# Starting the second layer of the first chunk early, and another order of weight scaling, in a Fourier-filter and snake-MLP kernel

## The chip, the cores and the metric

The kernel runs on one core of one Trainium2 chip. The metric is the device time of one execution in microseconds (us). An execution with the hardware profiler on gives the trace that the views below come from.

Engines: PE is TensorE (matmuls; PEld its weight loads), DVE is VectorE, ACT is ScalarE, POOL is GpSimd, SP is SyncE, which here only issues DMAs.

## The reference

Eight sequences of 3008 rows and 256 columns are filtered in the frequency domain, and all 24064 rows then go through an MLP with the snake activation:

```python
X = np.fft.rfft(x, axis=1)
y = np.fft.irfft(X * (filt_r + 1j * filt_i)[None], n=3008, axis=1)
h = y.reshape(24064, 256) @ w_in            # d_ff = 2048
g = h + sin(alpha * h) ** 2 / (alpha + 1e-09)
out = g @ w_out                             # float32
```

## The kernel before, in words

**Fourier part.** 3008 = 47 x 64, so the transform is two stages of small DFT matrices. Batch 0 is done in the head (L441 to L585). Batches 1 to 7 are done piece by piece between the MLP's matmuls: `first` (L206, PSUM tile pa; its copy to SBUF, t_h, by ACT or DVE in rotation), a round through DRAM (d<-t_h by SP, then t<-d, the t2 tiles, by POOL), `forward` (L243, pb), the product with the filter, `inverse` (pc), a second round through DRAM, and `last` (pd), whose result is y. For batch 1 there are sixteen pieces of `first`, called pa 0 to pa 15 here, and t_h k is the copy of pa k. In the trace, pa 0, 3, 6 and 9 are copied by DVE, the other twelve by ACT. The last step of batch 0 (`last_0`, L407, also called pd) is partly left for later: its matmuls are put one by one between MLP matmuls by `one_between`.

**MLP.** The rows are cut into 48 chunks of 512 columns of y (one in twelve has 384), and d_ff into 16 blocks jb of 128. With 2 sin^2 = 1 - cos(2 ...), the activation becomes v = cos(ph) - 1 - ph, where w_in is scaled by alpha beforehand (`weights_in`, six pieces g on POOL, L547) and w_out by -1/(2 alpha) (`weights_out`, three pieces of four blocks on POOL, L581, and four of one block on ACT, L579).

- `hidden(k, jb)` makes one block: two matmuls of 512 columns into ph (L608), cos on ACT into cos_all (L612), v on DVE (L613). Names such as ph 8, cos 8 and v 8 mean block jb = 8. There are four buffers of ph and four of cos.
- `project(k, u)` is the second layer: u = (t, half), where t is one of four tiles of 128 rows and half is blocks 0 to 7 or 8 to 15. It is eight matmuls of 256 columns into po (L628). Two tiles t share a PSUM bank; when both are done, ACT copies them to o (L637) and POOL issues the stores (L673).

**Order.** Each engine runs its instructions in program order. The program goes in half steps: `step` counts pairs of hidden blocks, eight per chunk. In step j of chunk k it emits `hidden(k, 2j)` and `hidden(k, 2j+1)`, then the Fourier pieces that `put` has laid on this step (`slot`), then 1/8 of the previous chunk's `project`. So chunk 0 has no second-layer work of its own beside it, and chunk 1 carries that of chunk 0.

**Buffers that matter here.** `fps` has two PSUM buffers, for pa, pb, pc and pd; `hps` four, for ph; `ops` two, for po. `vpool` has two buffers of SBUF: w_out32, the raw w_out, lies in the one that becomes v of chunk 1. `opool` has three: the zero tile `idle`, which feeds the idle matmuls of `warm_pe`, whose results nothing reads, and later the output tiles o.

**POOL's queue** from 29 to 47 us: w_in pieces 0 to 2, x load 0 of batch 1, w_in 3, x 1, w_in 4, x 2, w_in 5, x 3, then w_out blocks 0 to 3, 4 to 7 and 8 to 11. Blocks 12 to 15 are scaled on ACT from step 5 of chunk 0.

Of the kernel before, what the change touches and what calls it, by code (L numbers as in the profile page):

```python
# [10 lines left out]
FP32 = mybir.dt.float32  # L11
# [3 lines left out]
ALU = mybir.AluOpType  # L15
# [3 lines left out]
B, S, C = 8, 3008, 256  # L19
# [52 lines left out]
def kernel(  # L72
# [10 lines left out]
    nc = tc.nc  # L83
# [31 lines left out]
    opool = pool("op", 3)  # L115
# [4 lines left out]
    ops = pool("ops", 2, PSUM)  # L120
# [13 lines left out]
    y = cpool.tile([128, 2, 2, 32, NR], FP16)  # L134
# [4 lines left out]
    for h in range(2):  # L139
        (nc.sync, nc.scalar)[h].dma_start(out=x32[:, 4 * C * h:4 * C * h + 4 * C],  # L140
                                         in_=bass.AP(tensor=x.tensor, offset=x.offset + 4 * h * C, ap=[[32 * C, 96], [1, 4 * C]]))
# [5 lines left out]
    w2 = cpool.tile([128, 16, C], FP16)  # L147
# [34 lines left out]
    def evac(dst, src, on_act=None):  # L182
        flip[0] = (flip[0] + 1) % 3
        if flip[0] if on_act is None else on_act:
            marks["act"] = nc.scalar.copy(out=dst, in_=src)  # L185
        else:
            marks["dve"] = nc.vector.tensor_copy(out=dst, in_=src)  # L187
# [161 lines left out]
    def spread_alpha(i):  # L349

        ps = hps.tile([128, 4, 128], FP32, name=f"al_bc_{i}", tag="h")
        for a in range(4):
            for k, part in enumerate(parts):
                nc.tensor.matmul(out=ps[:, a, :], lhsT=one[:, 4 * i + a:4 * i + a + 1].to_broadcast([128, 128]),
                                 rhs=part, start=(k == 0), stop=(k == 2))
        nc.scalar.copy(out=alpha[:, i // 2, 512 * (i % 2):512 * (i % 2) + 512], in_=ps.rearrange("p a b -> p (a b)"))

    for g in range(2):
        gs = slice(12 * g, 12 * g + 12)
        for k, filt in enumerate((filt_r, filt_i)):  # L360
            for q in range(2):
                if (g, k, q) == (0, 1, 1):
                    split_alpha()
                off, step = ((12 * g) * C, C) if q == 0 else ((N1 - 12 * g) * C, -C)
                marks["filt", g, k] = nc.gpsimd.dma_start(
                    out=f_t[k][64 * k + 32 * q:64 * k + 32 * q + 32, gs, :],
                    in_=bass.AP(tensor=filt.tensor, offset=filt.offset + off,
                                ap=[[N1 * C, 32], [step, 12], [1, C]]))
        if g == 1:
            nc.gpsimd.tensor_copy(out=f_t[0][64:128, 0:12].rearrange("p s c -> p (s c)").bitcast(UINT32),  # L370
                                  in_=f_t[0][0:64, 0:12].rearrange("p s c -> p (s c)").bitcast(UINT32))
        nc.gpsimd.dma_start(out=e_t[:, gs, :], in_=e_dram.ap()[:, gs])

    idle = opool.tile([128, 512], FP32, name="idle", tag="o")
    nc.vector.memset(idle, 0.0)
    idle = idle.bitcast(FP16)
# [11 lines left out]
    rec_t = cpool.tile([128, 16], FP32)  # L388
# [8 lines left out]
    def last_0(n0, n, own=fps, tag="f", spread=False):  # L397

        for cb in range(2):
            made = []  # L400

            def one(i, cb=cb, made=made):

                if i == 0:
                    ps = own.tile([128, 512], FP32, name=f"pd_0_{n0}_{cb}", tag=tag)
                    made.append(ps[:, 0:n * NR].rearrange("p (a r) -> p a r", r=NR))
                nc.tensor.matmul(out=made[0][:, i, :], lhsT=t4_cols[:, n0 + i, :, cb], rhs=wi0_t,  # L407
                                 start=True, stop=True)
                if i == n - 1:
                    evac(y[:, cb, 0, n0:n0 + n, :], made[0], cb == 0)  # L410

            for i in range(n):
                if spread:
                    between.append(lambda i=i, one=one: one(i))
                else:
                    one(i)
# [7 lines left out]
    def inverse_table(g):  # L424

        gs = slice(8 * g, 8 * g + 8)
        ps = ops.tile([128, 8, 128], FP16, name=f"pse_{g}", tag="o")
        for i in range(8):
            for a in range(2):
                nc.tensor.transpose(out=ps[64 * a:64 * a + 64, i, :],  # L430
                                    in_=d_t[:, 8 * g + i, 64 - 64 * a:128 - 64 * a], identity=id16)
        nc.scalar.mul(e1_0[:, gs, :], ps, -0.125)
# [3 lines left out]
    def warm_pe(n):  # L436

        warmed.append(n)
        ps = hps.tile([128, 512], FP32, name=f"warm_{len(warmed)}", tag="h")
        for i in range(n):  # L440
            nc.tensor.matmul(out=ps, lhsT=idle[:, 0:128], rhs=idle[:, 0:512], start=True, stop=True)  # L441
# [18 lines left out]
    for i in range(16):  # L460
# [7 lines left out]
        if i < 15 and i % 4 == 3:  # L468
            warm_pe((1, 2, 2, 1)[i // 4])
    spread_alpha(0)  # L470
    [inverse_table(g) for g in range(2)]
    spread_alpha(1)
    warm_pe((2, 2, 2, 1)[3])
# [63 lines left out]
    nc.sync.dma_start(out=wh_t, in_=wh_dram.ap())  # L537
    nc.sync.dma_start(out=wi_t, in_=wi_dram.ap())
    w_out32 = vpool.tile([128, 16, C], FP32, name="w_out32", tag="v")
    for jb in range(0, 16, 8):  # L540
        ins = nc.sync.dma_start(out=w_out32[:, jb:jb + 8],
                                in_=moe_w_out[128 * jb:128 * jb + 1024].rearrange("(b p) c -> p b c", p=128))
    s1 = Spectral(1)

    def weights_in(g):
# [29 lines left out]

    def weights_out(jb, n=4):

        if n == 1:
            nc.scalar.mul(w2[:, jb, :], w_out32[:, jb, :], rec_t[:, jb:jb + 1])  # L579
        else:  # L580
            nc.gpsimd.tensor_tensor(out=w2[:, jb:jb + n, :], in0=w_out32[:, jb:jb + n, :],  # L581
                                    in1=rec_t[:, jb:jb + n, None].to_broadcast([128, n, C]), op=ALU.mult)

    spread_alpha(2)
    spread_alpha(3)  # L585
    for step in ([(weights_in, g) for g in range(3)] + [(s1.load_x, 0), (weights_in, 3), (s1.load_x, 1),
                 (weights_in, 4), (s1.load_x, 2), (weights_in, 5), (s1.load_x, 3)]
                 + [(weights_out, jb) for jb in (0, 4, 8)]):
        step[0](*step[1:])
    warm_pe(12)  # L590
    last_0(0, 4)
# [6 lines left out]
    v = {}  # L598
    pso = {}

    def hidden(k, jb):

        _, c0, n = chunks[k]
        if jb == 0:
            v[k] = vpool.tile([128, 16, 512], FP16, name=f"v_{k}", tag="v")
        ps = hps.tile([128, 512], FP32, name=f"ph_{k}_{jb}", tag="h")
        for cb in range(2):
            nc.tensor.matmul(out=ps[:, 0:n], lhsT=w1[:, cb, jb * 128:jb * 128 + 128],  # L608
                             rhs=y_cols[:, cb, c0:c0 + n], start=(cb == 0), stop=(cb == 1))
            one_between()  # L610
        cs = cos_all[:, jb % 4, :]
        nc.scalar.activation(out=cs[:, 0:n], in_=ps[:, 0:n], func=AFT.Sin, bias=float(np.pi / 2))  # L612
        marks["snake"] = nc.vector.scalar_tensor_tensor(  # L613
            out=v[k][:, jb, 0:n], in0=cs[:, 0:n], scalar=-1.0, in1=ps[:, 0:n],
            op0=ALU.add, op1=ALU.subtract)

    def project(k, u):

        pb, c0, n = chunks[k]
        t, half = divmod(u, 2)  # L620
        rest = len(chunks) - 1 - k
        alone = rest == 0 or rest == 1 and t > 1
        if rest == 0 and t > 1:
            t = 5 - t
        if (t % 2 == 0 or alone) and half == 0:
            pso[k] = ops.tile([128, 2, C], FP32, name=f"po_{k}_{t}", tag="o")
        for jb in range(8 * half, 8 * half + 8):
            nc.tensor.matmul(out=pso[k][:, t % 2, :], lhsT=v[k][:, jb, 128 * t:128 * t + 128],  # L628
                             rhs=w2[:, jb, :], start=(jb == 0), stop=(jb == 15))
            if jb % 2:  # L630
                one_between()
        last = 128 * (t + 1) == n
        if half == 1 and (t % 2 == 1 or last or alone):
            i0 = t % 2 if alone else 0
            o = opool.tile([128, 2, C], FP32, name=f"o_{k}_{t}", tag="o")
            copy = nc.vector.tensor_copy if rest == 0 else nc.scalar.copy
            copy(out=o[:, i0:t % 2 + 1, :], in_=pso[k][:, i0:t % 2 + 1, :])  # L637
            for i in range(i0, t % 2 + 1):
                store(o[:, i, :], pb, c0 + 128 * (t - t % 2 + i),
                      (nc.scalar, nc.sync, nc.scalar, nc.scalar) if rest == 0 and t == 3 else  # L640
                      (nc.sync, nc.scalar) if rest == 0 or (rest == 1 and t > 2) else
                      (nc.sync,) if rest < 7 else (nc.gpsimd,))
# [36 lines left out]
    def put(at, fn, *args, pe=False):  # L679
        pending.append((at, len(pending), pe, fn, args))  # L680
# [20 lines left out]
    for at, fn in put_later:  # L701
        put(at, fn)

    for jb in range(12, 16):
        put(5 + 0.5 * (jb - 12), weights_out, jb, 1)

    for n0, n, at in ((6, 5, 1.5), (11, 4, 11), (15, 4, 13), (19, 4, 14.4), (23, 4, 15.6), (27, 5, 16.8)):
        put(at, last_0, n0, n, fps, "f", True)
    for b in range(1, B):
# [46 lines left out]
    step = 0  # L756
    for k in range(len(chunks) + 1):
        for j in range(8):
            if k < len(chunks) and step > 0:
                hidden(k, 2 * j)  # L760
                hidden(k, 2 * j + 1)
            slot(step)
            if k > 0:
                n_half = 2 * (chunks[k - 1][2] // 128)
                for u in range(n_half * j // 8, n_half * (j + 1) // 8):
                    project(k - 1, u)
            slot(step + 0.5)
            step += 1
# [31 lines left out]
```

## Time and profile before

| | us |
|---|---|
| three runs: median (lowest, highest) | 773.94 (773.56, 774.11) |
| the profiled execution, its own time | 773.78 |
| its span in the trace | 772.0 |
| PE busy in the span | 762.5 (99%) |
| DVE, ACT, POOL busy | 655.7, 610.4, 373.4 |
| first matmul of chunk 0 (L608) starts | 35.10 |
| first second-layer matmul (L628) starts | 46.85 |
| first forward matmul of batch 1 (L243) starts | 69.72 |

A group of the page stands for instructions of one line and tile: `L608 PE MATMUL ph<-y,w ... x1536` is the first layer. In a timeline a row gives start, duration from the first start to the last end, engine, line, operation, tiles and count; the brackets at its end give idle time of the engine just before, and what ended it. The ends of matmuls are modelled and overlap the next start, so spacing tells PE's rate better than the duration of one record.

### The profile page before, as it was taken

How to read it: one execution, taken by the hardware profiler on the slowest of the kernel's cores; microseconds unless marked ns; L12 is line 12 of the kernel's file. 1: busy time of each engine (PE TensorE's matmuls, PEld its weight loads, DVE VectorE, ACT ScalarE, POOL GpSimd, SP SyncE). 2: the span in 40 equal slices, each digit the busy share in tenths (PEclk: the TensorE clock that was granted, in tenths of full speed). 3: DMA queues.
4: the chain of work that ended last, by engine and by line, in shares of the span. 5: the costliest groups of instructions: out<-in, count | busy, mean ns of one | idle time of the engine just before them, and what ended most of it. 6: DMA issues, size and time to landing. Idle time of an engine off the chain costs nothing.

```text
span 772.0 us, 17226 instructions
## 1 busy us (share of the span) xinstructions
PE 762.5 (99%) x6038; PEld 516.8 (67%) x6038; DVE 655.7 (85%) x1171; ACT 610.4 (79%) x1205; POOL 373.4 (48%) x651
## 2 busy tenths in 40 slices
PE   8999999999999999999999999999999999999997
PEld 4757766666666667666666676766666666766666
DVE  6887998999989888988889988899888888777774
ACT  5898987898787878887878787888778787777763
POOL 7455456544546555555555646644464645430000
PEclk9999999999999999999999999999999999999999
DMA  9955679754855438654575536754254322511112
GB/s 225 288 108 171 139 168 265 199 131 111 222 141 128 118 85 212 141 122 111 121 194 117 135 94 155 200 141 123 70 147 110 88 70 55 138 45 33 40 37 61
DMA packets 81518, 101.49 MB, mean 131 GB/s; under 512 B 18884, under 2 KB 60864, under 8 KB 81431
## 3 DMA queue, kind: packets, MB, share of 16 engines
q0 software_dynamic: 27440, 47.29, 26.1%
q1 hardware_dynamic: 53426, 52.41, 25.7%
q8 instruction: 47, 0.77, 0.4%
q10 hardware_dynamic: 565, 0.70, 0.3%
q14 instruction: 40, 0.33, 0.1%
HBM read 56.15 MB, written 46.66 MB: 133 GB/s over the span
## 4 chain that ended last, share of the span: by engine, by line
PE 92%; DVE 3%; ACT 2%; DMA 1%; issue 1%; POOL 0%; POOLq 0%
PE po L628 41%; PE ph L608 41%; DVE v L613 3%; PE pd L316 2%; PE pb L243 2%; PE pa L222 2%; DMA w<-id 1%; PE pc L293 1%; ACT xf L499 1%; ACT cos_all L612 1%; PE pa L206 0%; PE pc L518 0%; ACT t_h L185 0%; PE pd L407 0%; PE warm L441 0%
## 5 line engine op out<-in xcount | busy, mean ns | idle before, releaser
L613 DVE SCALAR_TENSOR_TENSOR v<-cos_all,ph 128x512 f16<-128x512 f32 (+1 forms) x768 | 482.8, 672 | 95.3 <-ACT cos_all L612 91.6
L612 ACT ACTIVATE cos_all<-ph 128x512 f32<-128x512 f32 (+1 forms) x768 | 413.8, 599 | 98.9 <-PE ph L608 98.6
L673 POOL DMA_DIRECT2D out_dram<-o x530 | 292.7, 559 | 241.8 <-ACT o L637 213.8
L608 PE MATMUL ph<-y,w 128*128 128x512 f16 (+1 forms) x1536 | 389.0, 375 | 1.3 <-DVE v L613 1.1
L628 PE MATMUL po<-w,v 128*128 128x256 f16 x3008 | 389.4, 273 | 0.0
L628 PEld LDWEIGHTS <-v 128*128 128x128 f16 x3008 | 290.0, 98 | 84.4 <-issue 1.1
L608 PEld LDWEIGHTS <-w 128*128 128x128 f16 x1536 | 143.2, 98 | 113.4 <-issue 18.4
L637 ACT COPY o<-po 128x512 f32<-128x512 f32 (+1 forms) x95 | 56.1, 590 | 7.6 <-PE po L628 6.8
L185 ACT CAST y<-pd 128x376 f16<-128x376 f32 (+1 forms) x86 | 41.9, 489 | 12.8 <-PE pd L316 8.8
L246 ACT CAST xf<-pb 128x512 f16<-128x512 f32 x84 | 50.9, 606 | 1.3 <-PE ph L608 0.5
L160 POOL DMA_DIRECT2D x<-in_x_dram x48 | 25.7, 540 | 40.8 <-DVE v L613 26.6
L185 ACT CAST t_h<-pa 128x512 f16<-128x512 f32 (+1 forms) x60 | 32.8, 590 | 12.5 <-PE pa L222 11.3
L316 PEld LDWEIGHTS <-t_a 96*128 96x128 f16 x448 | 31.4, 97 | 12.7
L264 DVE TENSOR_TENSOR p<-p,xs 128x512 f16<-128x512 f16 x84 | 35.7, 425 | 2.9
L263 DVE TENSOR_TENSOR xs<-xs,filt_t 128x512 f16<-128x512 f16 x84 | 35.2, 419 | 1.8 <-DMA xs<-xf 1.7
L257 DVE TENSOR_TENSOR p<-xf,filt_t 128x512 f16<-128x512 f16 x84 | 35.1, 419 | 0.0
L185 ACT CAST gt<-pc 128x512 f16<-128x512 f32 x54 | 28.1, 594 | 8.4 <-PE pc L293 8.4
L187 DVE CAST t_h<-pa 128x512 f16<-128x512 f32 (+1 forms) x52 | 33.5, 683 | 0.2
L243 PE MATMUL pb<-t,d_t 128*128 128x256 f16 x168 | 32.1, 273 | 0.0
L316 PE MATMUL pd<-wh_t,t_a 96*128 96x94 f16 x384 | 31.8, 204 | 0.0
L235 POOL DMA_DIRECT2D t<-d x28 | 24.4, 874 | 10.8 <-DMA d<-t_h 9.4
L243 PEld LDWEIGHTS <-d_t 128*128 128x128 f16 x168 | 16.4, 98 | 14.3
(71 smaller groups left out, 275.3 us busy)
## 6 DMA issues: line engine op xcount, KB each, us to landing
t<-d POOLq DMA_DIRECT2D x28, 384.0 KB, 5.2
xs<-xf SPq DMA_DIRECT2D x168, 64.0 KB
t_a<-d SPq DMA_DIRECT2D x28, 384.0 KB
x<-in_x_dram POOLq DMA_DIRECT2D x50, 188.0 KB, 4.5
d<-t_h SPq DMA_DIRECT2D x48, 192.0 KB
d<-gt SPq DMA_DIRECT2D x36, 256.0 KB
out_dram<-o POOLq DMA_DIRECT2D x91, 64.0 KB, 2.1
out_dram<-o POOLq DMA_DIRECT2D x31, 80.0 KB, 3.6
```

What stands on the lines that cost most here:

```text
L185: marks["act"] = nc.scalar.copy(out=dst, in_=src)
L243: nc.tensor.matmul(out=ps[:, i, :], lhsT=d_t[:, s, :], rhs=self.t2[s // 6][:, s % 6, :], start=True, stop=True)
L246: nc.scalar.copy(out=self.xf[u], in_=ps)
L263: nc.vector.tensor_tensor(out=xs, in0=xs, in1=f_t[1][:, 2 * u:2 * u + 2, :], op=ALU.mult)
L264: nc.vector.tensor_tensor(out=p, in0=p, in1=xs, op=ALU.add)
L316: nc.tensor.matmul(out=psv[:, i, :], rhs=wi_t if self.b < TILED else wh_t, start=True, stop=True, lhsT=t4_h[ch // 2][0:NK, n0 % 16 + i, cb ...
L608: nc.tensor.matmul(out=ps[:, 0:n], lhsT=w1[:, cb, jb * 128:jb * 128 + 128], rhs=y_cols[:, cb, c0:c0 + n], start=(cb == 0), stop=(cb == 1))
L612: nc.scalar.activation(out=cs[:, 0:n], in_=ps[:, 0:n], func=AFT.Sin, bias=float(np.pi / 2))
L613: marks["snake"] = nc.vector.scalar_tensor_tensor(out=v[k][:, jb, 0:n], in0=cs[:, 0:n], scalar=-1.0, in1=ps[:, 0:n], op0=ALU.add, op1=ALU. ...
L628: nc.tensor.matmul(out=pso[k][:, t % 2, :], lhsT=v[k][:, jb, 128 * t:128 * t + 128], rhs=w2[:, jb, :], start=(jb == 0), stop=(jb == 15))
L637: copy(out=o[:, i0:t % 2 + 1, :], in_=pso[k][:, i0:t % 2 + 1, :])
L673: queues[i % len(queues)].dma_start(out=bass.AP(tensor=out.tensor, offset=out.offset + t0 * C, ap=[*ap, [1, C]]), in_=o_blk[p0:p0 + rows, :])
```

## The change

1. **Second layer of chunk 0.** 24 of its 64 matmuls (blocks 0 to 5, all four t) move into chunk 0: after each of `hidden(0, 7)` to `hidden(0, 14)` three of them are emitted. Both PSUM tiles po of chunk 0 are opened there, each by one matmul of zeros over the whole bank (512 columns), since two row tiles now accumulate in a bank by turns. In chunk 1 the rest, 40 matmuls, is emitted as 4, 4, 0, 8, 8, 0, 8, 8 in the eight steps instead of 8 in each. The first copy to o comes in step 4 instead of step 3.
2. **w_out.** All its blocks are scaled on POOL, between the w_in pieces and x loads; the last four come in two pieces of two blocks, from tiles of their own in `opool`. Nothing of it is on ACT. It is loaded by four DMAs instead of two.
3. **y.** Of the `last_0` piece n0 = 6, both copies to y are on ACT; before, one was on DVE.
4. **Head.** Six idle matmuls after the first `spread_alpha`.

```diff
@@ last_0
-                    evac(y[:, cb, 0, n0:n0 + n, :], made[0], cb == 0)
+                    evac(y[:, cb, 0, n0:n0 + n, :], made[0], cb == 0 or n0 == 6)
@@ head
     spread_alpha(0)
+    warm_pe(6)
     [inverse_table(g) for g in range(2)]
@@ loads of w_out
-    for jb in range(0, 16, 8):
-        ins = nc.sync.dma_start(out=w_out32[:, jb:jb + 8],
-                                in_=moe_w_out[128 * jb:128 * jb + 1024].rearrange("(b p) c -> p b c", p=128))
+    w_out_rest = [opool.tile([128, 2, C], FP32, name=f"w_out_{jb}", tag="o") for jb in (12, 14)]
+    for jb, n, dst in ((0, 8, w_out32[:, 0:8]), (8, 4, w_out32[:, 8:12]), (12, 2, w_out_rest[0]), (14, 2, w_out_rest[1])):
+        nc.sync.dma_start(out=dst, in_=moe_w_out[128 * jb:128 * (jb + n)].rearrange("(b p) c -> p b c", p=128))
@@ weights_out: always nc.gpsimd.tensor_tensor; the ACT form for n == 1 is gone
@@ POOL's order
-    for step in ([(weights_in, g) for g in range(3)] + [(s1.load_x, 0), (weights_in, 3), (s1.load_x, 1),
-                 (weights_in, 4), (s1.load_x, 2), (weights_in, 5), (s1.load_x, 3)]
-                 + [(weights_out, jb) for jb in (0, 4, 8)]):
+    for step in ([(weights_in, g) for g in range(4)]
+                 + [(weights_out, 0), (s1.load_x, 0), (weights_in, 4), (s1.load_x, 1), (weights_out, 4),
+                    (weights_in, 5), (s1.load_x, 2), (weights_out, 8), (s1.load_x, 3), (weights_out, 12, 2), (weights_out, 14, 2)]):
@@ new
+    early = [(t, jb) for jb in range(6) for t in range(4)]
+
+    def project_early(n):
+
+        for _ in range(min(n, len(early))):
+            t, jb = early.pop(0)
+            if (t % 2, jb) == (0, 0):
+                pso[0, t // 2] = ops.tile([128, 2, C], FP32, name=f"po_0_{t}", tag="o")
+                nc.tensor.matmul(out=pso[0, t // 2].rearrange("p t c -> p (t c)"), lhsT=idle[:, 0:128],
+                                 rhs=idle[:, 0:512], start=True, stop=False)
+            nc.tensor.matmul(out=pso[0, t // 2][:, t % 2, :], lhsT=v[0][:, jb, 128 * t:128 * t + 128],
+                             rhs=w2[:, jb, :], start=False, stop=False)
@@ project
-        for jb in range(8 * half, 8 * half + 8):
+        for jb in range(8 * half if k or half else 6, 8 * half + 8):
@@ scaling on ACT
-    for jb in range(12, 16):
-        put(5 + 0.5 * (jb - 12), weights_out, jb, 1)
@@ main loop
-                hidden(k, 2 * j)
-                hidden(k, 2 * j + 1)
+                for jb in (2 * j, 2 * j + 1):
+                    hidden(k, jb)
+                    if k == 0 and jb > 6:
+                        project_early(3)
             slot(step)
-            if k > 0:
+            if k == 1:
+                for u in ((0, 2), (4, 6), (), (1,), (3,), (), (5,), (7,))[j]:
+                    project(0, u)
+            elif k > 0:
```

## Prediction

> **What bounds the kernel now.** I read the page first, then a table of stretches, then the chain of waits and the engines' timelines from 33 to 70 us, where the change lies. Of the page, part 1 (busy time) and part 4 (the chain that ended last):
>
> ```profile
> PE 762.5 (99%) x6038; PEld 516.8 (67%) x6038; DVE 655.7 (85%) x1171; ACT 610.4 (79%) x1205; POOL 373.4 (48%) x651
> PE 92%; DVE 3%; ACT 2%; DMA 1%; issue 1%; POOL 0%; POOLq 0%
> ```
>
> TensorE (PE) is the bound, so only a stretch in which PE waits can give time. The stretches, with the busy time of PE, its weight loads, DVE, ACT and POOL, the granted clock, the DMA share and GB/s:
>
> ```profile
> 40.00:50.00 10.00, 8.97 (x46) 4.47 (x46) 9.79 (x18) 9.46 (x20) 6.70 (x5) 1.00 0.54 88
> 50.00:60.00 10.00, 9.82 (x67) 6.41 (x65) 6.36 (x11) 9.11 (x19) 3.69 (x7) 1.00 0.50 144
> 400.00:600.00 200.00, 199.80 (x1606) 134.74 (x1604) 175.84 (x321) 161.36 (x321) 109.23 (x191) 1.00 0.53 131
> ```
>
> Late in the kernel PE has nothing to give. In chunk 0 (to about 47 us) VectorE (DVE) is full, and from 50 to 60 ScalarE (ACT) is at 9.11 of 10. The chain of waits there (start, us, what):
>
> ```profile
> 36.43 4.88 DVE v L613 x8
> 41.31 0.56 DVE y L187
> 41.87 3.60 DVE v L613 x6
> ...
> 45.99 0.60 ACT t_h L185
> 46.59 0.04 issue
> 46.63 0.38 PE pa L206
> 47.01 0.88 PE po L628 x8
> 47.88 0.22 PE pa L206
> 48.10 0.86 PE ph L608 x4
> ```
>
> The rates: ph and pa 0.216 us each (0.86 for 4), po 0.109, one v 0.60. A PE record ends 0.16 after its place in the stream. Two ACT operations in a row start 0.48 apart and last 0.60 each.
>
> **Part 1, the 24 early po.** From 39.48 (PE is through with ph 7) to 46.85 (first po) lie 7.37 us. PE's work in it is 16 ph (3.46), 3 pa (0.65), 4 ph of chunk 1 (0.87) and 2 pd (0.08), 5.06 in all: 2.31 us are idle. The change puts 24 x 0.109 = 2.62 and two zeroing matmuls, 0.43, into it: 3.05, more than the hole. A step of chunk 0 now costs PE 0.43 + 3 x 0.109 = 0.76 against 0.60 on DVE, so PE sets the pace, and reaches the same place at 39.48 + 8.11 = 47.60, 0.75 later. Chunk 1 loses 2.62. At most 2.62 - 0.75 = 1.87 us can be won.
>
> Step by step: the zeroing and three po stand between ph 7 and ph 8, so ph 8 starts at 40.24 (39.57 before); ph 15 ends in the stream at 46.08, cos 15 runs 46.27 to 46.87, v 15 to 47.59 (46.95 before). DVE's t_h of pa 0 then ends at 48.18 (47.55 before), pa 3 waits for it, and ph 2 of chunk 1 starts at 48.46 instead of 47.94: 0.52 **behind**.
>
> Chunk 1 then has 4, 4, 0, 8, 8, 0, 8, 8 po in its eight steps instead of 8 each. Steps 1 and 2 shed 12 x 0.109 = 1.31, so ph 6 starts near 51.55 (52.29 before), 0.74 ahead. Here ACT takes over: from 50.05 it has t_h 4, t_h 5, cos 4, cos 5, t_h 7, cos 6, cos 7, t_h 8 in a row, 8 x 0.48, the last done at 54.0. The first-stage products pa have two PSUM buffers, pa 8 waits for t_h 7 and pa 10 for t_h 8: ph 8 starts at 54.26 (54.80), 0.54 ahead. ACT before, in this place:
>
> ```profile
> 54.45 0.59 ACT L637 COPY o<-po 128x512 f32<-128x512 f32 x1
> ...
> 57.12 0.47 ACT L185 CAST y<-pd 128x376 f16<-128x376 f32 x1
> 57.50 1.14 ACT L185 CAST t_h<-pa 96x512 f16<-96x512 f32 x2
> 58.59 1.11 ACT L612 ACTIVATE cos_all<-ph 128x512 f32<-128x512 f32 x2
> 59.59 0.57 ACT L185 CAST t_h<-pa 96x512 f16<-96x512 f32 x1
> 60.63 0.59 ACT L185 CAST t_h<-pa 96x512 f16<-96x512 f32 x1 [0.46 <-PE pa L206]
> ```
>
> The copy o at 54.45 moves one step later, behind y. So ACT has y at 56.56, o, t_h 12 from 57.42 (57.50 before): 0.08 left of the 0.54. Then t_h 13, cos 10 at 58.50, cos 11 at 59.02, t_h 14 to 60.08. Before, eight po lay between pa 14 and pa 15; now pa 15 follows at once, waits for t_h 14 and starts at 60.14 (60.22). From there both programs issue the same work and PE is full. Part 1 gives **-0.08 us**: nearly all of the 1.87 is waited away on ACT. A handover is known to some 0.05 us and there are about ten in the chain, so I take -0.6 to +0.6 as its range.
>
> **Part 2, the ACT and DVE edits.** Four scalings of w_out leave ACT (42.49 and 44.24, 0.89 and 0.91 us). DVE waits there only 0.21 us, and PE's later pace covers that: 0. One y (0.56 on DVE) goes to ACT. Its last pd comes behind ph 8 at 40.92, ACT does it ahead of cos 8, and v 8 starts at 42.01 (41.79): what DVE saves it waits. 0, already in the walk.
>
> **Part 3, POOL's order.** Its rows before:
>
> ```profile
> 39.31 1.30 POOL L547 TENSOR_TENSOR w<-w_in,y 128x512 f16<-128x512 f32 x1
> 40.55 0.55 POOL L168 DMA_DIRECT2D x<-in_x_dram  x1
> 41.11 5.60 POOL L581 TENSOR_TENSOR w<-w_out,rec_t 128x1024 f16<-128x1024 f32 x3
> ```
>
> With 1.87 for a w_out piece, 1.83 and 1.30 for w_in, 0.55 for an x issue: piece 0 done at 37.8, x 0 issued at 37.8 (34.05 before), w_in 4 done 40.2, w_out 4 42.6, w_in 5 43.9, w_out 8 46.4, the last two (half a piece each, 0.95) 47.9 and 48.8. PE needs w_out 4 at 43.9, w_in 5 at 44.89, and the last blocks near 53: the smallest slack is 1.0 us. The x loads landed 5.0 to 6.8 us after issue: x 0 by 43.8 to 44.6, needed at 46.08. The first MB of w_out must be in SBUF by 35.9. The SyncE queue had moved 2.84 MB by 32 us and 3.43 by 34, of 4.29 in all; without w_out's second half that is 3.24, so 33.4. Chunk 1's first v overwrites w_out32, free at 46.4, needed at 48.1. SP issues two DMAs more, ahead of 19 idle us. All 0; were POOL's order late beyond 1.0 us, PE would wait one for one.
>
> **Part 4, the head.** Six idle matmuls, 6 x 0.216 = 1.29, go from 12.97 to 14.27 into this hole:
>
> ```profile
> 14.50 1.08 PE L430 MATMUL pse<-w,d_t 128*64 128x128 f16 x32 [1.36 <-DMA w<-id]
> ```
>
> The end of the wait is a DMA landing, so nothing moves: 0. The granted clock is 1.00 in every stretch there and PE's rows before and behind the hole have the full rate, so there is no rate to win; at worst, if the DMA were early, 0.3 us.
>
> [...] The chain shows ph at 0.216 us each, four in 0.86. [...]
>
> **The sum.** The profiled execution took 773.78 (span 772.0 and 1.78 around it), 0.16 under the median of the runs, 773.94. 773.78 - 0.08 = **773.7**.
>
> **Rivals.** *PE is bound throughout*: ACT's records overlap more than I reckon, or its waits fall where PE has po to run. For it: ACT's work between t_h 1 and t_h 15 is 26 x 0.48 = 12.5 us in a stretch of 15.2. Against it: two buffers and a fixed order. It gives the full 1.87: 771.9. Chance 0.14.
>
> *POOL is late*: the w_out DMAs land together at the queue's end, 37.5, not at 33.4. Everything of POOL moves 1.6, beyond the slack of 1.0: +0.6, 774.3. Against it are the queue's bytes. 0.06.
>
> *The reload of batch 1 becomes late* (the slower side). The t2 load was issued at 64.80 when the fourth d1 write had landed, landed 4.0 later, at 68.80, and its first matmul pb ran at 69.72: 0.92 us to spare. The moved copy o lets POOL start its seven stores near 57.5 (55.34 before), 3.69 us of issue, so that they run beside that write, issued at 61.2. If the write takes over 0.92 longer than its 3.6 us, PE waits for the rest; at double length 3.6 - 0.92 = 2.7, 776.4. Against it: the third write, at 57.06, ran beside the stores before, and its bytes were through by 60. 0.08.
>
> That the change does not do what it says is excluded by the instruction order of the changed program: the 24 po stand where it says.
>
> **The numbers.** Forecast 0.72 (773.1 to 774.4), PE bound 0.14, POOL late 0.06, reload late 0.08. Forecast and POOL make 0.78, so the range takes in the PE-bound case: 771.8 to 774.9. A measurement of this kernel tells about 0.2% (1.5 us) from no change: faster 0.14, same 0.78, slower 0.08.
>
> **What would show it.** Right: PE nearly without idle time from 39.5 to 47.5, v of chunk 0 ending near 47.6; PE waits for ACT t_h at pa 8, 10, 12, 13 and above all 15, 1 us there; ph 12 of chunk 1 at 60.4 as before. Wrong: ph 12 of chunk 1 near 58.5, which is the PE-bound case; a wait of PE for POOL in chunk 0; a PE wait ahead of the first pb, near 69.6; a granted clock under 1.00 in the head.

## The result, and the profile after

The changed kernel takes 775.83 us (median of 14 runs, 775.06 to 777.09), the kernel before, on the same chip, 774.06 (14 runs, 773.56 to 776.18). The ratio on record, which is not the quotient of the two medians, is 1.0019, 95% interval 1.0013 to 1.0026: slower by 0.2%, where 773.7 (771.8 to 774.9) was forecast. The profiled execution took 775.95, its span 774.1, which is 2.14 us more than before's.

Parts 1 and 4 of the page after, as they were shown of before:

```profile
PE 763.5 (99%) x6046; PEld 517.6 (67%) x6046; DVE 655.6 (85%) x1170; ACT 610.1 (79%) x1202; POOL 374.1 (48%) x653
PE 88%; DMA 4%; ACT 3%; DVE 2%; issue 1%; POOL 1%; SPq 0%; POOLq 0%
```

PE is as full as before, but the chain that ended last now runs through DMA for 4% of the span instead of 1%. The stretches (busy time of PE, weight loads, DVE, ACT, POOL, then clock, DMA share, GB/s):

```profile
40.00:50.00 10.00, 9.97 (x63) 6.15 (x62) 8.98 (x15) 8.43 (x17) 8.93 (x9) 1.00 0.89 146
50.00:60.00 10.00, 8.99 (x54) 5.28 (x53) 6.92 (x12) 9.43 (x20) 1.81 (x4) 1.00 0.45 129
400.00:600.00 200.00, 199.80 (x1604) 134.61 (x1603) 175.63 (x322) 161.70 (x322) 107.79 (x189) 1.00 0.52 130
```

The change did what it says: PE went from 8.97 to 9.97 of 10 in the first stretch. The second took it back, 9.82 to 8.99, with ACT at 9.43. These are the PE rows there that show a wait (the bracket: idle time ahead of the row, and what ended it):

```profile
57.45 0.38 PE L206 MATMUL pa<-x,wf_t 94*96 94x512 f16 x1 [0.18 <-ACT y L185]
58.41 0.20 PE L407 MATMUL pd<-wi_t,t_a 128*128 128x94 f16 x1 [0.37 <-ACT t_h L185]
60.50 0.38 PE L206 MATMUL pa<-x,wf_t 94*96 94x512 f16 x1 [0.89 <-ACT t_h L185]
```

The last is pa 15, the wait that the prediction put first. The first is pa 13; it waits 0.18 for y, as in before. The pd in the middle shares its PSUM buffers with pa and waits for the copy t_h 12.

To see where the 2.14 us came from, I laid the 768 cos of ACT of both traces side by side: the offset of the i-th cos changes only where time is lost or won. It was +0.29 at the first cos, the same +0.29 at the end of chunk 1, and then rose by 0.56 at the first pb (70 us), by 0.89 near 142, by 0.13 near 530; the tail behind the last cos was 0.27 longer. Together these five are the 2.14. So on balance nothing was lost where the work was changed. The chain of waits after, at the first rise (d<-t_h is a write of the first round through DRAM, called a d1 write here, t<-d the load back, the t2 load):

```profile
61.52 4.44 DMA d<-t_h
...
66.03 0.51 issue
...
66.55 3.97 DMA t<-d
...
70.57 0.39 PE pb L243 x2
```

The t2 load is issued 5.03 us behind the fourth d1 write; before it was 3.56. That is the "reload late" rival, in its place, and PE's wait ahead of the first pb is one of the prediction's own signs of being wrong. The rest of the study asks why the write is late, and why other transfers are.

### The profile page after: what moved, and what is told of

Read it like the earlier page. It is cut to its first block, busy times and chain, and to the rows that moved or that the text cites. A ratio compares the mean times of both kernels' runs of the same rounds, so it can differ in the third digit from the quotient of the medians.

```text
span 774.1 us, 17238 instructions
## 1 busy us (share of the span) xinstructions
PE 763.5 (99%) x6046; PEld 517.6 (67%) x6046; DVE 655.6 (85%) x1170; ACT 610.1 (79%) x1202; POOL 374.1 (48%) x653
## 4 chain that ended last, share of the span: by engine, by line
PE 88%; DMA 4%; ACT 3%; DVE 2%; issue 1%; POOL 1%; SPq 0%; POOLq 0%
PE po L642 39%; PE ph L607 39%; PE pb L243 2%; PE pd L316 2%; DVE v L612 2%; PE pa L222 2%; DMA w<-id 1%; DMA d<-t_h 1%; PE pc L293 1%; DMA x<-in_x_dram 1%; ACT cos_all L611 1%; ACT t_h L185 1%; ACT xf L500 1%; DMA t<-d 1%; PE pc L519 0%
```

## The experiments

Sixteen kernels ran, in fours on one chip with runs of before beside them. "Reload" is the time from the issue of the fourth d1 write to that of the first t2 load, "loss" the rise of the offset at the first pb. The times and ratios are of 7 to 12 runs of each kernel (the ratios as on record, not quotients of the medians; in the first four's runs of before, three took 779.9 to 782.4). The last three columns are read from one profiled execution each.

| kernel | median us | before there | ratio, interval | reload | loss | DVE's wait for xs at 522 |
|---|---|---|---|---|---|---|
| after_again | 775.52 | 774.18 | 1.0023 (1.0014 to 1.0032) | 4.96 | 0.45 | 0.76 |
| late_copy | 776.15 | 774.18 | 1.0019 (1.0001 to 1.0037) | 5.16 | 0.61 | 0 |
| no_early | 774.92 | 774.18 | 1.0001 (0.9977 to 1.0024) | 4.99 | 0.66 | 0.65 |
| no_warm | 775.08 | 774.18 | 1.0013 (1.0004 to 1.0021) | 3.75 | 0 | 0.78 |
| before_again | 774.17 | 773.84 | 1.0006 (0.9996 to 1.0015) | 3.56 | 0 | 0 |
| six_only | 774.73 | 773.84 | 1.0011 (0.9999 to 1.0024) | 4.95 | 0.37 | 0 |
| parts_2_3 | 774.48 | 773.84 | 1.0012 (1.0004 to 1.0021) | 3.55 | 0 | 1.03 |
| after_24 | 775.77 | 773.84 | 1.0032 (1.0018 to 1.0045) | 3.72 | 0 | 0.77 |
| three_00 | 774.90 | 774.30 | 1.0014 (1.0005 to 1.0023) | 3.55 | 0 | 0.93 |
| three_01 | 776.51 | 774.30 | 1.0027 (1.0015 to 1.0040) | 4.92 | 0.57 | 0.69 |
| three_10 | 775.36 | 774.30 | 1.0014 (1.0005 to 1.0022) | 3.89 | 0 | 0.68 |
| three_11 | 774.69 | 774.30 | 1.0015 (1.0000 to 1.0030) | 5.02 | 0.45 | 0.75 |
| act_pad | 774.54 | 774.28 | 1.0005 (0.9995 to 1.0015) | 3.55 | 0 | 0.35 |
| pad_split | 774.01 | 774.28 | 0.9997 (0.9989 to 1.0006) | 3.56 | 0 | 0.18 |
| early_pad | 775.25 | 774.28 | 1.0012 (1.0003 to 1.0021) | 3.77 | 0 | 0.35 |
| full_pad | 774.52 | 774.28 | 1.0005 (0.9996 to 1.0014) | 4.47 | 0 | 0.21 |

### First four: undo one part at a time

The theories: the moved copy's stores run beside the fourth write (the prediction's mechanism); accidents of DMA timing; the new order of loads and scalings; the idle matmuls delay the head. `after_again` is the changed kernel once more, the others:

```diff
@@ late_copy: the first copy to o one step later still
-                for u in ((0, 2), (4, 6), (), (1,), (3,), (), (5,), (7,))[j]:
+                for u in ((0, 2), (4, 6), (), (1,), (), (5,), (3,), (7,))[j]:
@@ no_early: all second-layer matmuls of chunk 0 in chunk 1, as before
-                    if k == 0 and jb > 6:
-                        project_early(3)
@@ no_warm
-    warm_pe(6)
```

> The changed kernel once more, to see which of its three losses recur: +0.29 us in the head (the identity table landed later), +0.56 at the first forward matmul of batch 1 (the t2 reload landed at 70.52, PE was there at 70.15), +0.89 near 142 us (an x load landed 8.1 us after its issue). Theory A: the moved copy of o puts seven stores beside the fourth d1 write, so the wait at the first forward matmul recurs (0.3 to 0.8 us), and the loss near 142 us follows in most executions because DMA traffic of batch 2 is in the same phase; median 775.4 to 776.2. Rival B: all three are accidents of DMA timing in one execution; then the median is 775.8 all the same, but the profile shows the losses at other places.

> The order of the second layer of chunk 0 in chunk 1 becomes 4, 4, 0, 8, 0, 8, 8, 8, with the third tile before the second: the first copy of o and its stores come behind the t2 loads on GpSimd, the copy is no longer between y and t_h 12 on ScalarE, and eight po lie between pa 14 and pa 15. Theory A: the d1 write takes 3.6 us instead of 4.4, the wait at the first forward matmul goes (-0.6 us), and the wait of 0.9 us at pa 15 goes too; together 774.2 to 774.9, or 773.4 to 774.0 if the loss near 142 us goes with them. Rival C (the losses come from the new order of loads and scalings on GpSimd and SyncE, not from the stores): the wait at the first forward matmul stays; 775.0 to 775.8.

> The changed kernel without the early second layer: project of chunk 0 runs in chunk 1 as before; order of GpSimd, four loads of w_out, y on ScalarE and the six idle matmuls stay. Theory A: the stores start where they did before, no wait at the first forward matmul, no loss near 142 us: 773.7 to 774.5, the kernel before within 0.1%. Rival C: the loss stays, 775.2 to 776.0.

> The changed kernel without the six idle matmuls in the head. By the trace PE waits there for a DMA landing in both kernels, so all theories here expect no difference: 775.4 to 776.2, within 0.1% of the changed kernel. Rival D (the idle matmuls delay the head, whose chain was 0.29 us later): 775.5 or less by 0.3 us, seen as an earlier first matmul of chunk 0.

The late reload is no accident of one execution: `after_again` has it too (4.96). The loss near 142 did not come again there. The stores are not it either. In `late_copy` no store stands beside the write (the later copy costs 0.8 in chunk 1 by itself), in `no_early` they stand as early as before (54.98), and both reloads take 5 us. The POOL rows of before, of the changed kernel and of `no_early` (idle time ahead in the bracket):

```profile
64.80 3.35 POOL L235 DMA_DIRECT2D t<-d  x4 [5.78 <-DMA d<-t_h]
```

```profile
66.55 3.34 POOL L235 DMA_DIRECT2D t<-d  x4 [4.70 <-DMA d<-t_h]
```

```profile
65.87 3.35 POOL L235 DMA_DIRECT2D t<-d  x4 [7.22 <-DMA d<-t_h]
```

And only the kernel without the six idle matmuls is at 3.75. Its head was 0.24 late all the same and that of `after_again` 0.10 early: the shift at the first cos is chance of a DMA, not the idle matmuls.

The single DMA packets of the trace then showed what differs. The page after counts two queues of instruction packets (packets, MB, share):

```profile
q8 instruction: 47, 0.77, 0.4%
q14 instruction: 40, 0.33, 0.1%
```

q8 moves packets of 16384 bytes, mostly 0.9 to 1.4 us each, one for some 128 matmuls (6046 / 47); its 0.77 MB is 64 bytes for each of the 2 x 6046 matmuls and weight loads. So I take them for PE's own instructions, an estimate from these counts. q14 moves 8192 bytes at a time; its 0.33 MB is again 64 bytes for each of the other 5146 instructions of the page (of 17238), so I take it for the instructions of ACT, DVE, POOL and SP together. A packet of either queue is called a fetch here. The fourth d1 write has 96 packets of 4096 bytes, sixteen of 4 bytes, called completion packets here, and sixteen landings; the t2 load is issued 0.59 us behind the last of these in before (64.21, 64.80) and after (65.96, 66.55). In the changed kernel, at this write:

```
q8 packet                 63.94 to 64.86
last completion packet    64.85      (the fifteenth: 64.50)
landings                  ... 64.40  64.56  64.93  65.96
before: q8 packet 63.35 to 64.31, last completion packet 63.86, last landing 64.21
```

The reading: one fetch got onto a DMA engine between the write's last 4 KB and its completion packet there, and the write counts as landed 1.03 us later than its other fifteen parts. That is **theory E**. The trace does not name a packet's DMA engine; that the two share one is read from the times, since the completion packet begins 14 ns before the fetch ends. PE itself shows no wait there (busy 2.00 of 2 us from 63 to 65).

### Theory E against the order of loads

```diff
@@ six_only: before, and in the head
+    warm_pe(6)
@@ parts_2_3: no_early without its warm_pe(6)
@@ after_24: the changed kernel, first idle matmuls
-    warm_pe(12)
+    warm_pe(36, 128)      # 128 columns each
```

> The kernel before, unchanged, for a second trace. New theory E: on DMA queue q8 ('instruction'), 47 times in a run, a packet of 16384 bytes and 0.92 to 0.96 us is moved, one about every 128 matmuls, so these are TensorE's own instructions. Where one stands on a DMA engine in front of the last packet of a transfer of queue q1, the transfer lands about 1 us later (changed kernel: fetch 63.94 to 64.86, the 4-byte completion packet at 64.85, the sixteenth landing 65.96 against 64.93 for the fifteenth). In the first trace of before no such hit fell on q1. E: the place of the fetch in the program is the same, so the stage from the fourth d1 write to the t2 load is again near 3.6 us (under 4.2). Theory B (accident of each execution): 3.7 or 5.0, either. Time 774.1, ratio 1.000.

> The kernel before with the six idle matmuls in the head alone. E: the fetches move six matmuls earlier in TensorE's program (as in the run without the early second layer, which had six more matmuls than before and was hit at 63.26), the stage from the fourth d1 write to the t2 load takes 5.0 us instead of 3.6, TensorE waits 0.4 to 0.7 us more near 70 us; time 774.5 to 775.2. Theory C (POOL's order and the loads are the cause): the stage is as before, 3.6, and the time 774.1. Theory D (idle matmuls delay the head): cos 0 later than 35.8, nothing near 70.

> The changed kernel without the early second layer and without the six idle matmuls: as many matmuls as before, in the same order; only w_out, its loads, POOL's order and one y are changed. E: the fetches stand as in before, the stage takes about 3.7 us, nothing is lost near 70, and the 0.2 us that these parts win in chunks 0 and 1 stay: 773.7 to 774.2, ratio 0.9995 to 1.000. Theory C: the stage takes 5.0 and 0.6 us go near 70: 774.7 to 775.

> The changed kernel, with the first twelve idle matmuls of 512 columns made into 36 of 128: 24 matmuls more at no more columns, so that the fetches come 24 matmuls, some 4 us, earlier at 64 us, between the third and the fourth d1 write. E: the stage takes 3.6 to 3.8 us instead of 5.0, nothing is lost near 70 us, and ph 12 of chunk 1 to the first pb is as in before; other transfers may be hit later, so the whole time is less sure, 774.2 to 775.5. Theories B and C: the stage stays at 5.0 and the time at 775.7.

All four reloads came out as E has it: 3.56, 4.95, 3.55, 3.72. Six idle matmuls alone, added to before in a hole of PE, make the reload 1.4 us longer (fetch 63.86 to 64.83, completion packet at 64.82). The new order of loads does not (3.55). With 24 matmuls more the fetch comes at 60.85 to 61.79, ahead of the write, and the loss is gone. As for whole times, `after_24` and `parts_2_3` missed their expectations, and `parts_2_3` stayed 0.6 above before: its trace loses 0.22 in the head, 0.65 near 144 us, 0.46 near 530 and 0.27 in the tail, and gains 0.20 in chunk 0. A loss of 0.4 to 0.6 is 0.05 to 0.08%, less than most of the intervals tell apart; E rests on the traces, not on the times.

One thing in E's expectations did not come. Twelve instructions more ahead of it should bring the fetch earlier, by about 1 us at 0.2 us a matmul. In `six_only` it begins 2.36 us behind the issue of the write, in before 2.10, so it came 0.26 later; only the 24 more of `after_24` brought it forward, from 2.42 behind the issue to 1.28 ahead of it. That the idle matmuls move the fetch is shown, how they do is not.

The profiled run of `after_24` (781.77, the slowest of its twelve) also shows two long waits. It lost 6.4 us near 144, where pa waited 1.10 and 2.42 us for x; the stretches around it (the clock is the third figure from the end):

```profile
140.00:145.00 5.00, 1.81 (x13) 0.92 (x11) 1.93 (x4) 2.19 (x5) 1.56 (x3) 0.89 0.99 267
145.00:150.00 5.00, 4.67 (x22) 2.30 (x23) 3.10 (x6) 2.15 (x4) 4.13 (x8) 0.50 0.62 120
150.00:155.00 5.00, 5.00 (x36) 3.27 (x34) 3.37 (x7) 3.57 (x8) 2.08 (x4) 0.93 0.55 165
155.00:160.00 5.00, 5.00 (x44) 3.49 (x45) 4.68 (x10) 4.08 (x8) 1.87 (x4) 1.00 0.43 73
```

Behind these two waits, 3.5 us together, the granted clock is 0.50 for five us and 0.93 for the next five: the 6.4 us lost are nearly twice the 3.5 of waiting. Around the one shorter wait there in the changed kernel (0.50) it is 1.00 in every stretch from 138 to 160.

### The tail, and the two parts crossed

In every kernel with 401 DMAs of SP and ACT (before has 399) the tail was 0.27 to 0.36 longer. **Theory F**: these DMAs take eight semaphores by turns, and at the end SP tests them in the same order in before and after, 0.06 us each (in after the last eight tests start from 772.81 to 773.24). The last store of before has the seventh; the sixth of nine tests, for a store just ahead of it, is the one that waits, and three follow. With 401 it has the first; the second test waits, and seven follow. Four runs load w_out by three DMAs, 400 in all, with and without the idle and the early matmuls:

```diff
@@ three_00 (neither), three_01 (six idle), three_10 (24 early), three_11 (both)
-    for jb, n, dst in ((0, 8, w_out32[:, 0:8]), (8, 4, w_out32[:, 8:12]), (12, 2, w_out_rest[0]), ...
+    for jb, n, dst in ((0, 12, w_out32[:, 0:12]), (12, 2, w_out_rest[0]), ...
```

> The changed kernel without the early second layer and without the six idle matmuls (as the run parts_2_3), and w_out's first twelve blocks loaded by one DMA: 400 DMAs of SP and ACT instead of 401, 399 before. Theory F, the tail: these DMAs take eight semaphores by turns, and at the end SP tests them one after another, 0.06 to 0.07 us each. The last store of before has the seventh of them (three tests still follow its landing in the trace), with 401 DMAs the first (seven tests follow: +0.27), with 400 the eighth: two tests or fewer follow, tail -0.05 to -0.2 against before, about -0.4 against parts_2_3. E: as many matmuls as before, no fetch in front of the fourth d1 write's last packet, stage 3.6 to 4. Time 773.5 to 774.1, ratio 0.999 to 1.0005. Rival to F (the tail is chance, or set by the longer program): tail +0.27 again.

> As three_00, with the six idle matmuls in the head. E: fetch in front of the last packet of the fourth d1 write, t2 load about 1.2 us later than in three_00 (stage 5.0), 0.4 to 0.6 us lost near 70 us; time 0.4 to 0.8 above three_00. If idle matmuls cost nothing: as three_00.

> As three_00, with the 24 early matmuls of the second layer and the two of zeros (two matmuls more at 63 us than before). E: no hit, stage 3.6 to 4. The walk: they cost 0.2 in chunk 0 and 1 against three_00 (the 0.19 that the other parts win is given back) and no more: 0.1 to 0.3 above three_00. Rival, that the early matmuls cost something beyond that later (their copies and stores move): 0.5 or more above three_00.

> The whole change with w_out in three DMAs. E and F: the hit near 63.9 and its 0.5 us as in the changed kernel, tail 0.3 to 0.45 shorter than there; time 775.0 to 775.5, the sum of the two above. If the parts do not add (a hit that depends on more than the count of matmuls): below 774.6.

E: reloads of 3.55, 4.92, 3.89 and 5.02, late with the idle matmuls only. F: two tests follow the landing in all four, and three tails are -0.06, 0.00 and -0.07; in `three_00` the landing itself came 0.28 later, +0.21. The four times all lie outside what was expected of them and can't be added up, because the larger w_out load brought losses of its own, and the trace of `three_10` lost 2.05 ahead of the first cos. In `three_00`, POOL:

```profile
36.41 1.90 POOL L578 TENSOR_TENSOR w<-w_out,rec_t 128x1024 f16<-128x1024 f32 x1 [0.60 <-DMA w_out<-in_moe_w_out_dram]
```

This is the prediction's rival "POOL is late", made true by another edit: 0.42 us go in chunks 0 and 1 there, 2.5 in `three_01`.

### The loss near 530, and the early matmuls by themselves

At 522 us DVE waits for a transfer xs<-xf (from one SBUF tile to another, for the product with the filter), with its v queued behind, in ten of eleven kernels without ACT's four scalings (the expectation below says eight of nine), and in none of the three whose ACT program is that of before. The row of before, then that of `parts_2_3`:

```profile
521.37 0.43 DVE L263 TENSOR_TENSOR xs<-xs,filt_t 128x512 f16<-128x512 f16 x1
```

```profile
522.98 0.42 DVE L263 TENSOR_TENSOR xs<-xs,filt_t 128x512 f16<-128x512 f16 x1 [1.03 <-DMA xs<-xf]
```

**Theory G**: without the scalings ACT has five instructions less, and a packet of q14 comes later. Put on the clock of before by the cos around it, it stands at 510.5 to 510.6 in those three and at 513.3 to 513.8, beside the xs transfers, in all eleven (so in `late_copy` too, which has no wait). The test gives ACT five tiny copies in the first 7 us, where it is idle; a table loaded in eight pieces makes 408 DMAs, for F:

```diff
@@ act_pad: parts_2_3 with
+    for i in range(5):
+        nc.scalar.copy(out=warm, in_=warm)
@@ pad_split (act_pad), early_pad (no_warm with the copies), full_pad (the changed kernel with the copies), each with
-    nc.sync.dma_start(out=wi_t, in_=wi_dram.ap())
+    for i in range(8):      # behind w_out
+        nc.sync.dma_start(out=wi_t[12 * i:min(12 * i + 12, NK)], in_=wi_dram.ap()[12 * i:min(12 * i + 12, NK)])
```

> The changed kernel without early second layer and without idle matmuls (as parts_2_3), with five more ACT copies of a 128x1 tile in the first 7 us, where ACT has nothing to do: as many instructions on PE and on ACT as before. Theory G: queue q14 moves the instructions of ACT, DVE, POOL and SP in packets of 8192 bytes; without ACT's four scalings (2405 instructions instead of 2410) the packet that comes at 510.4 us in before comes near 514, among the xs transfers, and DVE waits 0.65 to 1.03 for them at 522 (in eight of nine changed kernels, in none of the three whose ACT program is that of before). With the five copies: packet back near 510.5, no wait of DVE for xs at 522, no loss near 530, none near 70; the tail +0.27 stays. Time 773.7 to 774.4. Rival (the loads or POOL's order cause the late xs): wait of 0.65 to 1 again.

> As act_pad, and one table of 96 rows loaded by eight DMAs of 12 rows, behind w_out: 408 DMAs of SP and ACT, so that the last store has the eighth of the eight semaphores. F: tail 0 to -0.2 against before, as in three of the four runs with 400 (-0.06, 0.00, -0.07, and 0.21 in the fourth). With G: 773.4 to 774.0, ratio 0.999 to 1.000. Rival to F: tail +0.27.

> The whole change without the six idle matmuls, with the five ACT copies and the split table. E, F and G: no loss near 70, none near 530, tail 0 to -0.2; chunks 0 and 1 as the walk has them, 0.0 to 0.2 behind pad_split: 773.6 to 774.3. Rival (the early matmuls cost something by themselves later): 0.5 or more above pad_split.

> The whole change with the five ACT copies and the split table. E: the fetch near 63.9 and the t2 load 1.2 us later are there again, 0.4 to 0.6 us lost near 70; G and F: nothing near 530, tail 0 to -0.2. 774.2 to 774.9, 1 us less than the changed kernel. If one cause lies behind both places: neither loss.

F again: two tests follow the landing in the last three, tails -0.06 and -0.07 in two; in `pad_split` the landing came 0.38 later, +0.31. G holds in these traces: the packet is back at 510.5 to 510.8 in all four, and nothing is lost near 530. The same row in `act_pad`:

```profile
521.50 0.43 DVE L263 TENSOR_TENSOR xs<-xs,filt_t 128x512 f16<-128x512 f16 x1 [0.35 <-DMA xs<-xf]
```

A wait of 0.2 to 0.35 stays, so the packet is not all of it, but PE no longer feels it. Five copies that compute nothing take the loss away.

`full_pad` missed its expectation in an instructive way: no loss at 70, with the six idle matmuls in it. Its fetch came at 64.25 to 65.19, 3.0 us behind the write instead of 2.4, just after the last completion packet (64.25). So "six idle matmuls, late reload" is no rule, "fetch in front of the completion packet, late reload" is: in seven traces of eighteen the last completion packet begins 14 to 15 ns before the fetch ends, and these took 4.92 to 5.16; in the other eleven it does not, and they took 3.55 to 4.47. The 4.47 of `full_pad` costs nothing because it is within the 0.92 to spare (3.56 + 0.92 = 4.48). What moved the fetch by those 0.6 us is open; the split table adds seven DMAs and some instructions to PE's program. Nor does the time of the fetch alone decide: in `act_pad` and `early_pad` it comes 2.39 and 2.42 behind the write's issue, as in the changed kernel, two completion packets begin after it, and nothing is delayed. Which DMA engine a fetch gets may decide it; the trace does not tell.

`full_pad`, the whole change with three side effects out of the way (one of them by that unforeseen shift of the fetch), is 0.24 us above before by medians, against 1.77 for the change itself; the intervals, 0.9996 to 1.0014 and 1.0013 to 1.0026, just touch. `pad_split`, without early and idle matmuls, is the best: 0.9997 (0.9989 to 1.0006), not to be told from before. The early matmuls cost 0.18 to 0.20 in chunks 0 and 1 (offset 0.00 with them, -0.18 to -0.20 in the four kernels without them that load w_out by four DMAs). Whether they cost more later isn't settled. By medians they do: `full_pad` is 0.5 above `pad_split` and `early_pad`, which missed its expectation, 1.2, and 0.5 was the mark set for that rival. But the trace of `early_pad` loses 0.5 in the head and 1.0 near 340, places that other kernels with and without early matmuls lose at in some executions.

## Why the prediction was wrong, point by point

**The walk of part 1 was right.** Forecast: -0.08 by the end of chunk 1; measured: 0.00, in the changed kernel and in seven more with the early matmuls in the same order. Allowing for the 0.29 of the head, v of chunk 0 was to end at 47.88, and does (start, duration, and the wait ahead of it):

```profile
42.33 5.55 DVE L612 SCALAR_TENSOR_TENSOR v<-cos_all,ph 128x512 f16<-128x512 f32 x8 [0.73 <-ACT cos_all L611]
```

The wait before pa 15 was put at 1 us and is 0.89. A step of chunk 0 takes PE 0.76 us as worked out, with 0.216 us for each ph (steps start at 41.05, 41.81 and 42.56).

**"From there both programs issue the same work and PE is full" failed.** The same work was issued, but not with the same landing times of its DMAs. Of the 2.14 us of the trace, the study gives a cause for 0.56 (70 us), 0.13 (530) and 0.27 (the tail); 0.29 is a shift of the head that goes either way from execution to execution, and for the 0.89 near 142, the largest, no cause is shown. (0.28 of the distance from 773.7 to 775.83 is the base: the sum started from one execution of 773.78, and the median of fourteen is 774.06.) Three of the terms put at nothing were not nothing:

- *Part 4, "nothing moves: 0".* The six matmuls do fill the hole and delay nothing directly. PE after:

```profile
13.15 1.46 PE L441 MATMUL warm<-idle 128*128 128x512 f16 x6
14.79 1.08 PE L430 MATMUL pse<-w,d_t 128*64 128x128 f16 x32 [0.19 <-DMA w<-id]
```

But they add twelve instructions to PE's program, and with them the fetch near 64 us stood in front of a completion packet in seven traces of nine, and 0.37 to 0.66 us went at 70 us; without them in none of nine.
- *Part 2, "0".* In chunk 0 that was nearly right (0.18 to 0.20 won where the early matmuls don't take it up). But ACT's shorter program moves a fetch on q14: 0.08 to 0.46 near 530 us in ten traces of eleven.
- *Part 3, "SP issues two DMAs more ... All 0".* No wait of PE for POOL came, so the slacks were right. With the two DMAs seven of the last semaphore tests instead of three follow the one that waits: 0.27.

**The rival "reload late"** had the place and the point from which it decides: with 0.92 us to spare and a reload 1.47 later, the first pb was 0.56 later (1.47 - 0.92 = 0.55), and the trace shows 0.42 of it as PE's wait. Its mechanism, the stores, was wrong (with the early matmuls and no such fetch the reload took 3.72 to 4.47, within the spare time), its price (2.7) too high, and its chance, 0.08, far too low, because it was judged by the stores alone. A slack of 0.92 us on a transfer seen in one execution was taken for safe.

**What stays open.** The 0.89 us near 142: `after` and `after_24`, `six_only`, `parts_2_3` and `late_copy` lose 0.6 to 6.4 there, the others 0.14 or nothing; `after_again`, the same kernel as `after`, loses nothing. From 120 to 128 us the DMA engines are full (share 0.9 or more in nearly every slice, in before too) with d1 writes, x loads and stores; the t2 load follows the last of them at 128.3 in before and at 128.9 to 131.7 in those five, but at 129.3 to 129.9 in three that lose nothing there. In the changed kernel a completion packet begins 14 ns before a PE fetch ends there (129.66 to 130.61), and in `late_copy` one 11 ns before (128.97 to 130.01); but so it does in `before_again`, which loses nothing, and in the other three of the five none does. So fetches are a part of it at most. Executions of one kernel differ as much by themselves: before took 773.3 to 777.1, but for the three at 779.9 to 782.4. And `no_warm`, `early_pad` and `full_pad`, all with the early matmuls, lose 0.23 to 0.51 near 110 us; in `no_warm` the chain there runs through a transfer xs<-xf that landed at 105.45. Why it was late was not studied.

## What to carry to other kernels

In this kernel, whose bound engine is 99% busy, a change of the instruction count of PE or ACT, even by instructions that compute nothing, moved packets of instructions against the transfers of the run: with six idle matmuls the reload came 1.4 us later (`six_only`), with five tiny copies on ACT the wait at 522 us went from 1.03 to 0.35 (`act_pad`). For other kernels that is a reason to look, not a result. List the transfers with less than about 1.5 us of slack (the reloads here came 1.0 to 1.5 later) and see, in the trace, how far the nearest fetch packet is from their last packets. Before a loss of 0.1 to 0.2% is blamed on the change itself, run it with the instruction and DMA counts padded back.

## What the runs showed of the hardware

- A fetch packet of 16384 bytes mostly took 0.9 to 1.4 us. A completion packet that began 14 ns before the end of one landed 1.1 us after its own start (64.85 to 65.96 in the changed kernel), where the last one of before took 0.35 (63.86 to 64.21). What holds it up for that time is not shown by any run here.
- After waits of 1.10 and 2.42 us close together (the second ended at 145.33) PE's granted clock was 0.50 from 145 to 150 us (`after_24`).
- At the end of the program SP spent 0.06 us on each semaphore test. Three of the nine tests stood behind the one that waited in before, seven in the changed kernel, and two behind the landing in the seven runs with 400 or 408 DMAs of SP and ACT.
